# One core, one launch: a linear-attention scan and a gated feed-forward under a new order of work, with the flag of the general path tested early

## The chip, the cores and the metric

The kernel runs on one core of one Trainium2 chip. The core has a matrix engine (TensorE, "PE" in the profile, its weight loads "PEld"), a vector engine (VectorE, "DVE"), an activation engine (ScalarE, "ACT"), a general engine (GpSimd, "POOL") and a sync engine (SyncE, "SP"), which here issues all DMAs. Each engine runs its own list of instructions in order; they meet by semaphores. The metric is the device time of one execution in microseconds, and lower is better.

## The reference, cut to what matters

Eight heads of a gated linear attention with a complex decay, then a feed-forward block with a token shift and a sigmoid gate:

```python
mag = np.sqrt(a_re * a_re + a_im * a_im)
scale = np.minimum(mag, 0.999) / (mag + 1e-06)
a_re_n, a_im_n = (a_re * scale, a_im * scale)
for t in range(S):                       # S = 768, B = 4, H = 8, D = 48
    new_re = ar * S_re - ai * S_im       # ar, ai: row t of a_re_n, a_im_n
    new_im = ar * S_im + ai * S_re
    S_re, S_im = (new_re + k_t (x) v_t, new_im)
    y[:, :, t] = q_t . S_re
x_prev = x shifted by one token          # x = y, heads side by side: 384 wide
xk = mu_k * x + (1 - mu_k) * x_prev
xr = mu_r * x + (1 - mu_r) * x_prev
k = np.maximum(xk @ w_k, 0.0)            # 384 -> 1024
v = k * k @ w_v                          # 1024 -> 384
r = 1.0 / (1.0 + np.exp(-(xr @ w_r)))
return r * v
```

## The kernel before, in words

The sequence of each of the 4 batches is cut into two units of 384 tokens, so there are 8 units, u = 0 to 7. A unit passes through three stages.

The gate stage (`gate`, phase "g") loads the decays, keys and queries (`g<-in_gat`) and values (`v<-in_vt`), and turns the decays into cumulative logarithms and phases on ACT and DVE: exponentials, logarithms, arctangent, sine, two scans. The results multiply keys and queries in place (`g<-g,sq`, L712, and `g<-g,r`, L757). On the way the last columns and sums go into a tile `stat` (copies L705 and L731, accumulations of ACT): they show whether the decays stay in the range in which this way of computing is exact.

The attention stage (`attend`, phase "a") transposes keys on PE (`tr`, L848; L912 in unit 0), copies them out on ACT (`kt`), forms the products of keys and values per 64 tokens (`up`, L881; L951 in unit 0), adds them up to states on DVE, forms scores within 64 tokens (`sc`, L998, L993), masks them on DVE (`pt`) and sums both parts into the output (`y`, L1039). ACT writes that to the unit's input of the feed-forward, `xt` (L1074), and small DMAs move the last heads' rows (`xt<-ys`).

The feed-forward stage (`mix`, phase "m") forms the two mixes of neighbouring tokens (`x`, L376 and L380 in unit 0), the gates (`z` with `zr` by ACT), the first projection (`z`, L421, L417 in unit 0), its squared ReLU (`r`, `h`, `hx`), the second projection (`o`, L506), and the product of gate and projection (`y<-o,zr`, L524), which SP stores (`out_t<-y`, L529). In all units but the first a float32 operand is split in two parts and each block takes three matmuls. In unit 0 the weights, which come packed (phases "f": fetch `raw`, "w": convert with `hx<-raw` L574 and `wx` L579, "s": split), are used whole.

Phase "x" holds 48 steps of two matmuls on a tile of zeros (`room<-idle`, L1128), whose result nobody reads. The first 25 steps have widths of 512 to 256 columns, the others 384.

No loop orders the work. Each step registers itself with what it reads and writes, and a table `ORDER` gives each step of each phase its place in one list of 1652 steps. `Plan.run` sorts by the places, checks that each step stands behind what it depends on, and emits them; so the table sets the order on each engine's list, on the DMA queue of SP, and in which buffer a tile lies (`HOMES`). Nothing is scheduled after that.

After the list the kernel compares `stat` with limits (`lim`, written by memsets of POOL at the end), sums the comparisons over partitions by a matmul (`n`, L1168), writes an integer flag `bad` (L1169), loads it into a register of each engine (`nc.values_load`, L1172) and branches on it (L1173). Where the flag is set, a slow general path computes everything again, token by token; with these inputs it isn't set, and the branch jumps over that code.

Of the kernel before, what the change touches and what calls it, by code (L numbers as in the profile page):

```python
# [13 lines left out]
I32 = mybir.dt.int32  # L14
# [155 lines left out]
}  # L170
PIECE = 2
HB = 2
XB = 3
GB = 2
VB = 4
# [1098 lines left out]
```

## Time and profile before

| what | us |
|---|---|
| median of 3 runs (lowest to highest) | 408.85 (408.64 to 409.87) |
| the profiled execution: its time | 409.39 |
| its span, first to last instruction | 407.6 |
| time around the span | 1.79 |
| PE busy | 385.6 (95% of the span), 5801 matmuls |
| DVE busy, ACT busy | 319.2 (78%), 312.9 (77%) |
| mean granted clock of PE | 0.971 of 2.4 GHz |

The busy time of PE is counted from modelled ends of matmuls that overlap, so a busy PE isn't a PE at its peak. Times in the rows are microseconds from the span's start. In a row of busy shares each digit stands for a fortieth of the span, about 10.2 us. "Idle before" names what ended an engine's wait; "issue" means that nothing in the profile ended it.

### The profile page before, as it was taken

Reading aid. Unit: us, or ns where it says so; the run is one execution under the profiler, and the core shown is the slowest. Engines: PE = TensorE matmul, PEld = TensorE weight load, DVE = VectorE, ACT = ScalarE, POOL = GpSimd, SP = SyncE. Lnnn points to the kernel's source line nnn. Section 1 sums busy time; section 2 is a strip of 40 time slices with the busy share of each in tenths; the row PEclk is TensorE's granted clock in tenths of the full one; section 3 lists DMA queues with packets and bytes.
Section 4 is the critical chain, followed back from the end, with each engine's and each line's share of the span. In section 5 each row is a group of like instructions: output and inputs, shape, how many; then the busy total and the mean of one; then the engine's idle time right before and its main releaser. Section 6 shows DMA issues by size and latency. Waiting matters only on the chain.

```text
span 407.6 us, 13560 instructions
## 1 busy us (share of the span) xinstructions
PE 385.6 (95%) x5801; PEld 352.1 (86%) x5801; DVE 319.2 (78%) x516; ACT 312.9 (77%) x617; POOL 8.8 (2%) x32
## 2 busy tenths in 40 slices
PE   7769999999999999999999999999999999999993
PEld 6658865686798989999999989999999998999992
DVE  2996889899998799988997889969886955444352
ACT  6998999999999789899996988699767634152430
POOL 6000000000000000000000000000000000000000
PEclk9955999999999999999999999999999999999998
DMA  7987491514553515454144643344311332100101
GB/s 269 414 285 185 150 357 59 125 42 143 179 146 97 219 45 127 159 181 92 34 126 132 191 110 112 84 160 121 65 62 46 67 82 50 37 0 2 58 1 65
DMA packets 22994, 49.70 MB, mean 122 GB/s; under 512 B 4848, under 2 KB 16368, under 8 KB 22928
## 3 DMA queue, kind: packets, MB, share of 16 engines
q1 hardware_dynamic: 22928, 48.78, 39.2%
q8 instruction: 47, 0.77, 0.8%
q14 instruction: 19, 0.16, 0.1%
HBM read 31.06 MB, written 4.72 MB: 88 GB/s over the span
## 4 chain that ended last, share of the span: by engine, by line
PE 85%; DVE 6%; ACT 3%; issue 2%; DMA 2%; SPq 0%; DVEq 0%; ACTq 0%
PE z L421 28%; PE o L506 24%; PE y L1039 9%; PE sc L998 6%; PE up L881 5%; PE z L417 5%; PE tr L848 3%; DVE g L757 2%; PE sc L993 2%; PE up L951 1%; PE tr L912 1%; PE room L1128 1%; DMA g<-in_gat 1%; DMA xt<-ys 1%; DVE ph L722 1%
## 5 line engine op out<-in xcount | busy, mean ns | idle before, releaser
L421 PE MATMUL z<-x,w 128*128 128x384 f32 x693 | 127.3, 338 | 0.0
L421 PEld LDWEIGHTS z<-x,w 128*128 128x128 f32 x693 | 120.0, 188 | 1.2 <-ACT zr L285 0.2
L506 PE MATMUL o<-hx,w 128*128 128x384 f32 x504 | 96.0, 340 | 0.8 <-issue 0.7
L506 PEld LDWEIGHTS o<-hx,w 128*128 128x128 f32 x504 | 86.8, 188 | 2.1 <-issue 1.0
L278 ACT ACT_TABLE_LOAD x37 | 47.5, 1283 | 1.5 <-PEq L1263 0.8
L757 DVE TENSOR_TENSOR g<-g,r 128x768 f32<-128x768 f32 (+1 forms) x24 | 41.8, 1755 | 8.5 <-ACT r L285 7.9
L463 ACT ACTIVATE r<-z 128x384 f32<-128x384 f32 x64 | 31.0, 492 | 14.7 <-PE z L421 11.4
L467 ACT ACTIVATE h<-r 128x384 f32<-128x384 f32 x64 | 33.5, 528 | 9.4 <-DMA out_t<-y 4.7
L479 DVE TENSOR_TENSOR hx<-h,hx 128x384 fp32r<-128x384 f32 x56 | 30.5, 554 | 2.0 <-ACT hx L473 1.0
L394 ACT CAST x<-xm 128x384 fp32r<-128x384 f32 x42 | 21.3, 518 | 11.8 <-DVE xm L386 9.1
L397 DVE TENSOR_TENSOR x<-xm,x 128x384 fp32r<-128x384 f32 x42 | 22.9, 552 | 8.3 <-ACT x L394 8.0
L475 DVE CAST hx<-h 128x384 fp32r<-128x384 f32 x44 | 15.5, 355 | 17.5 <-PE o L506 9.8
L285 ACT ACTIVATE sq<-m 128x1152 f32<-128x1152 f32 (+1 forms) x30 | 28.1, 968 | 1.3 <-DVE m L681 1.2
L998 PE MATMUL sc<-g 48*64 48x64 f32 x1200 | 26.9, 234 | 0.8 <-issue 0.7
L998 PEld LDWEIGHTS sc<-g 48*64 48x64 f32 x1200 | 24.4, 143 | 3.4 <-issue 2.2
L891 DVE TENSOR_TENSOR state<-up,state 112x384 f32<-112x384 f32 x35 | 19.4, 553 | 9.4 <-PE up L881 8.2
L1074 ACT ACTIVATE xt<-y 112x192 f32<-112x192 f32 (+2 forms) x36 | 14.3, 396 | 15.4 <-PE y L1039 13.9
L1039 PE MATMUL y<-q,state 112*64 112x64 f32 (+1 forms) x704 | 25.3, 227 | 0.7 <-issue 0.7
L1039 PEld LDWEIGHTS y<-q,state 112*64 112x64 f32 (+1 forms) x704 | 23.0, 134 | 3.3 <-issue 2.3
L386 DVE SCALAR_TENSOR_TENSOR xm<-dx,mu_sb,xt 128x384 f32<-128x384 f32 x42 | 25.5, 614 | 0.4
L285 ACT ACTIVATE zr<-z 128x384 f32<-128x384 f32 x24 | 11.3, 490 | 17.2 <-PE z L421 17.2
L881 PEld LDWEIGHTS up<-v,kt 64*48 64x48 f32 (+1 forms) x1216 | 20.9, 127 | 3.7 <-issue 1.5
(87 smaller groups left out, 582.9 us busy)
## 6 DMA issues: line engine op xcount, KB each, us to landing
g<-in_gat SPq DMA_DIRECT2D x18, 768.0 KB, 6.5
raw<-in_w_all SPq DMA_DIRECT2D x9, 767.8 KB, 8.2
g<-in_gat SPq DMA_DIRECT2D x12, 384.0 KB, 4.4
v<-in_vt SPq DMA_DIRECT2D x24, 192.0 KB, 3.1
out_t<-y SPq DMA_DIRECT2D x24, 192.0 KB, 2.0
q<-g SPq DMA_DIRECT2D x84, 48.0 KB, 2.3
q<-g SPq DMA_DIRECT2D x28, 144.0 KB, 2.9
q<-g SPq DMA_DIRECT2D x40, 72.0 KB, 2.8
```

The lines of the kernel that those rows point to most:

```text
L278: nc.scalar.add_instruction(mybir.InstLoadActFuncSet(name=nc.get_next_instruction_name(), act_func_set_id=n, engine=mybir.EngineType.Activ ...
L285: nc.scalar.activation(out=out, in_=in_, func=func, **kw)
L386: nc.vector.scalar_tensor_tensor(out=xm[which, ct], in0=d[ct], scalar=mu_sb[:, which, ct:ct + 1], in1=X[u][:, ct, 0:U], op0=ALU.mult, op1= ...
L421: nc.tensor.matmul(z, lhsT=wt[s[0]][:, part, s[1]], rhs=r[which][:, ct], start=n == 0, stop=n == 3 * NT - 1)
L463: nc.scalar.activation(out=t["r", j], in_=t["f", j], func=AF.Relu, scale=1.0 / W_SCALE)
L467: nc.scalar.activation(out=t["h", j], in_=t["r", j], func=AF.Square)
L479: nc.vector.tensor_tensor(out=t["lo", j], in0=t["h", j], in1=t["hi", j].bitcast(F32), op=ALU.subtract)
L506: nc.tensor.matmul(tiles["o", mt], lhsT=w, rhs=r, start=j == 0 and n == 0, stop=j == NJ - 1 and n == len(parts) - 1)
L757: nc.vector.tensor_tensor(out=g[:, d, 2 * i:2 * i + 2], in0=g[:, d, 2:4], in1=t["r"][:, 1 - i, d].unsqueeze(2).to_broadcast([P, k, 2, U]), ...
L881: nc.tensor.matmul(t["up", c, s][i * HR:(KR if i else HR), h * D:(h + 1) * D], lhsT=keys, rhs=V[u][c][r, h * D:(h + 1) * D], start=True, s ...
L998: nc.tensor.matmul(y, lhsT=g[:, 2 * i, q], rhs=g[:, 2 * i + 1, q], start=i == 0, stop=i == 1)
L1039: nc.tensor.matmul(t["y", team][s][rows, h // 2 - team[0], c], lhsT=lhsT[:, cols], rhs=rhs, start=(s, h % 2) not in begun, stop=stop)
```

## The change

It does three things.

First, `ORDER` and `HOMES` are other numbers throughout: the list has three steps more, and nearly every step has another place in it. One line of the table before and after:

```diff
-    ("x", 0): (21, 26, 29, 32, 36, 40, 43, 46, 48, 51, 53, 55, 56, 58, 62, 64, 67, 69, 70, 72, 74, 76, 78, 82, 84, 87,
+    ("x", 0): (66, 77, 69, 25, 182, 84, 92, 102, 56, 269, 75, 41, 74, 110, 32, 46, 272, 37, 136, 82, 145, 98, 175, 63,
```

The fill steps are no longer in the order of their widths. On PE, at the start (`tr`, `sc`, `up`: the attention of unit 0), the list was:

```order
L912 MATMUL tr<-ident,g 128x128 x6
L998 MATMUL sc<-g 64x64 x24
L951 MATMUL up<-v,kt 64x48 x2
...
L951 MATMUL up<-v,kt 48x48 x2
L912 MATMUL tr<-ident,g 128x128 x3
L998 MATMUL sc<-g 64x64 x24
L912 MATMUL tr<-ident,g 128x128 x9
L951 MATMUL up<-v,kt_316 64x48 x2
```

and is now:

```order
L924 MATMUL tr<-ident,g 128x128 x6
L1010 MATMUL sc<-g 64x64 x24
L924 MATMUL tr<-ident,g 128x128 x3
L1140 MATMUL room<-idle 128x320 x2
L1140 MATMUL room<-idle 128x384 x2
L1140 MATMUL room<-idle 128x512 x2
...
L963 MATMUL up<-v,kt 64x48 x2
...
L963 MATMUL up<-v,kt 48x48 x2
L1140 MATMUL room<-idle 128x384 x4
L924 MATMUL tr<-ident,g 128x128 x9
```

Ahead of these rows stand 70 fill matmuls in both lists. Of the other 26, two, 14 and 10 stood in three groups, two behind the first `y` product, 14 ahead of the last one and 10 behind it; now there are groups of eight, four, two and two in this stretch, none until the last `y` of unit 0, and 10 behind it, ahead of the first feed-forward.

On ACT, where the sines of unit 0 end and the first keys are copied out (`r` are phases, `kt` transposed keys, `hx<-raw` a weight conversion), the list was:

```order
L745 ACTIVATE r<-r 128x384
L285 ACTIVATE r<-r,half_pi 128x384
L919 COPY kt<-tr 128x384
L926 COPY kt_316<-tr 128x3x2x16
L574 CAST hx<-raw 128x768
```

and is now:

```order
L757 ACTIVATE r<-r 128x384
L586 CAST hx<-raw 128x768
L290 ACTIVATE r<-r,half_pi 128x384
L290 ACTIVATE r<-r 128x384
L757 ACTIVATE r<-r 128x384
L931 COPY kt<-tr 128x384
```

One conversion has moved from behind the first copy of keys to a place ahead of it.

Second, the test of `stat` becomes steps of the list (phase "z": `look`), and the copies into `stat` are free to stand anywhere ahead of it. When 40 steps of the list are left, all of the last feed-forward, the flag is loaded on every engine and a branch hint is placed with it. On PE, near the end of the last unit, the list was:

```order
L421 MATMUL z<-x,w 128x384 x9
L506 MATMUL o<-hx,w 128x384 x3
L1168 MATMUL n<-ones_79,good 1x1
L1172 TENSOR_LOAD bad
L1173 COMPARE_AND_BRANCH
```

and is now:

```order
L1174 MATMUL n<-ones_79,good 1x1
L518 MATMUL o<-hx,w 128x384 x9
L433 MATMUL z<-x,w 128x384 x18
L518 MATMUL o<-hx,w 128x384 x9
L1184 TENSOR_LOAD bad
L1291 BRANCH_PREFETCH_HINT
L518 MATMUL o<-hx,w 128x384 x27
L433 MATMUL z<-x,w 128x384 x9
L518 MATMUL o<-hx,w 128x384 x24
L433 MATMUL z<-x,w 128x384 x18
L518 MATMUL o<-hx,w 128x384 x3
L1194 COMPARE_AND_BRANCH
```

The load and the hint now stand 81 matmuls ahead of the branch.

Third, the limits are written at the program's start, by ten memsets of POOL that stand ahead of the memset of `idle`, and a scratch size for DMA descriptors is set smaller.

```diff
 PIECE = 2
+LOAD = 40
+HINTED = (mybir.EngineType.PE, mybir.EngineType.DVE, mybir.EngineType.Activation, mybir.EngineType.SP, mybir.EngineType.Pool)
...
             emit()
             done.add(i)
+            if self.late and len(order) - len(done) == self.late[0]:
+                assert all(self.ops[j][2][0] == "m" for j in range(len(order)) if j not in done)
+                self.late[1]()
...
     nc.gpsimd.memset(ones1, 1.0)
+    lim = keep.tile([P, 2, ST_ALL], F32, name="lim")
+    for lo, hi, a, e in ((-2.0 ** 100, 2.0 ** 100, ST_X, ST_SQ), (0.0, 2.0 ** 20, ST_SQ, ST_L),
+                         (L_MIN, L0, ST_L, ST_PHI), (0.0, 1.0 / RE_MIN, ST_RE, ST_ALL),
+                         (-64.0, 64.0, ST_PHI, ST_RE)):
+        nc.gpsimd.memset(lim[:, 0, a:e], lo)
+        nc.gpsimd.memset(lim[:, 1, a:e], hi)
+    bad = keep.tile([1, 1], I32, name="bad")
     idle = keep.tile([P, 512], F32R, name="idle")
...
+        flag = []
+
+        def look():
+            good = keep.tile([P, 1], F32, name="good")
+            t, sn = {}, slot("ps")
+
+            def test():
+                ok = keep.tile([P, 2, ST_ALL], F32, name="ok")
+                nc.vector.tensor_tensor(out=ok[:, 0], in0=stat, in1=lim[:, 0], op=ALU.is_ge)
+                nc.vector.tensor_tensor(out=ok[:, 1], in0=stat, in1=lim[:, 1], op=ALU.is_le)
+                nc.vector.tensor_reduce(out=good, in_=ok, axis=mybir.AxisListType.XY, op=ALU.add)
+
+            def total():
+                t["n"] = bank(sn, "n")[:1, :1]
+                nc.tensor.matmul(t["n"], lhsT=good, rhs=ones1, start=True, stop=True)
+
+            def judge():
+                nc.vector.tensor_single_scalar(out=bad, in_=t["n"], scalar=2.0 * P * ST_ALL - 0.5, op=ALU.is_lt)
...
+        def load():
+            flag.append(nc.values_load(bad, min_val=0, max_val=1))
+            tc.mark_branch_hint_location("general", flag[0], engines=HINTED)
+
+        run([look], ("z", 0))
         with tc.manual_schedule():
             load_table(6)
+            plan[0].late = LOAD, load
             plan[0].homes = HOMES
             plan[0].run(ORDER)
...
-    flag = nc.values_load(bad, min_val=0, max_val=1)
-    with tc.If(flag > 0):
+    with tc.If(flag[0] > 0, label="general"):
...
-    nc = bacc.Bacc("TRN2", target_bir_lowering=False, num_devices=1)
+    nc = bacc.Bacc("TRN2", target_bir_lowering=False, num_devices=1, dynamic_dma_scratch_size=8192)
```

## Rows read from the trace of the kernel before

**Rows 1.** The page: busy tenths of PE and DVE in 40 slices.

```profile
PE   7769999999999999999999999999999999999993
DVE  2996889899998799988997889969886955444352
```

**Rows 2.** Stretches: length, busy of PE, PEld, DVE, ACT, POOL, clock, DMA share, GB/s.

```profile
24.31:51.57 27.26, 25.16 (x592) 21.95 (x593) 21.97 (x48) 24.41 (x53) 0.00 (x0) 0.67 0.62 176
...
53.28:400.72 347.44, 342.51 (x5126) 314.01 (x5125) 279.22 (x436) 266.21 (x516) 1.97 (x14) 1.00 0.35 102
```

**Rows 3.** Waits of PE, 53.28 to 400.72: total us, times, longest.

```profile
PE y L1039 <- issue: 1.6, 3, 0.7
PE z L417 <- DVE x L380: 0.9, 1, 0.9
PE sc L998 <- issue: 0.7, 1, 0.7
PE o L506 <- issue: 0.7, 1, 0.7
PE tr L848 <- DVE g L757: 0.6, 1, 0.6
PE z L417 <- DVE state L891: 0.2, 1, 0.2
```

**Rows 4.** Stretches of one microsecond, columns as in Rows 2.

```profile
22.00:23.00 1.00, 0.00 (x0) 0.00 (x0) 1.00 (x2) 1.00 (x4) 0.00 (x0) 0.52 1.05 424
42.00:43.00 1.00, 1.00 (x32) 0.93 (x33) 0.90 (x5) 1.00 (x4) 0.00 (x0) 0.74 0.17 68
```

**Rows 5.** Timeline of PE at the start: start, length, instructions, idle before.

```profile
2.65 15.09 PE L1128 MATMUL room<-idle 128*128 128x512 f32 x70 [2.65 <-POOL idle L328]
23.37 0.90 PE L912 MATMUL tr<-ident,g 128*128 128x128 f32 x3 [5.63 <-DVE g L757]
```

**Rows 6.** The chain that ended last: start, length, what, instructions.

```profile
31.55 2.12 PE tr L912 x9
...
35.98 2.09 PE y L1039 x41
38.07 0.94 PE room L1128 x2
...
44.64 1.22 PE y L1039 x38
...
47.64 2.64 PE room L1128 x14
...
189.15 1.31 PE tr L848 x12
```

**Rows 7.** The branch at line 1173: ns shortest/median/longest, start.

```profile
L1173 ACTq COMPARE_BRANCH  x1: 50/50/50, 401.9 to 401.9; - x1
...
L1173 PEldq COMPARE_BRANCH  x1: 3802/3802/3802, 402.0 to 402.0; - x1
```

**Rows 8.** The flag's load at line 1172, columns as in Rows 7.

```profile
L1172 DVEq TENSOR_LOAD <-bad x1: 545/545/545, 401.4 to 401.4; - x1
L1172 PEldq TENSOR_LOAD <-bad x1: 487/487/487, 401.4 to 401.4; - x1
```

**Rows 9.** Timeline of DVE at the end: the last product.

```profile
400.76 0.56 DVE L524 SCALAR_TENSOR_TENSOR y<-o,zr 128x384 f32<-128x384 f32 x1
```

**Rows 10.** DMA issues from 395 us on: KB each, median us to landing.

```profile
out_t<-y SPq DMA_DIRECT2D x3, 192.0 KB, 1.9
```

**Rows 11.** Groups by line: the weight conversion, busy us, mean ns.

```profile
L574 ACT CAST hx<-raw 128x768 f16<-128x768 bf16 (+1 forms) x10 | 10.1, 1023 | 0.0
```

**Rows 12.** Groups by line: one of the two lines of limits.

```profile
L1160 POOL MEMSET lim<- 128x24 f32 (+2 forms) x5 | 0.6, 133 | 16.7 <-PE sc L998 16.7
```

**Rows 13.** Timeline of POOL at the start: the statistics' zeroing.

```profile
2.54 0.27 POOL L331 MEMSET stat<- 128x208 f32 x1
```

**Rows 14.** Timeline of ACT at the start: the first accumulation.

```profile
5.38 0.52 ACT L285 ACTIVATE ph<-m 128x384 f32<-128x384 f32 x1
```

More of the change, by code (lines that the diff above doesn't have):

```diff
@@ L194 @@
     "g": "01010101",
-    "hx": "0100101010101010010010101010101010101010100110101010110101",
-    "kt": "001010010110110101101101",
+    "hx": "0110101010101010100101010111010101101011010010010100101101",
+    "kt": "010101010101110010110101",
     "ps": (
-        "400123230221232413134014143002041302310304102042111343104224341042421031010420124323313402434013"
-        "014302023040411232421032111301314213012410403232424032402434314013101232042120342034233010201342"
-        "32430042302411334102410101240432032124310344014304113044130324"
+        "320123321041320241400442323024023024211431223030440131423030134324243420241342031340303120123402"
+        "321301213113030044204230400340213400230442340112301204130134314022023142410313030341411321421040"
+        "010243121324043143243120132211331013342402340243104042324020314"
     ),
-    "pt": "01000110100101100101100110011010",
+    "pt": "01001001100110100110100101010110",
     "r": (
-        "021301201230131210102123032103210310203021131320211320312230302031231023123223010112130310211220"
-        "21031032030132100203313112310123200230321130203103203102"
-    ),
-    "v": "120310023102103021301210",
-    "x": "021011122021200011201012022102102022120102022102120011021021102",
+        "023110210231022303112102021102102102010212031312120301202101030210230012303031101212203210132001"
+        "30231031212130112030212303021013021221331033213021321203"
+    ),
+    "v": "130201312102130021301021",
+    "x": "021011201210211201211021022102200120022100210210210200210201200",
 }
@@ L219, in __init__ @@
     def __init__(self):
-        self.ops, self.data, self.slots, self.phase, self.homes = [], {}, {}, None, {}
+        self.ops, self.data, self.slots, self.phase, self.homes, self.late = [], {}, {}, None, {}, {}
     def slot(self, tag):
@@ L1147, in tile_kernel @@
                 run(gate(u + 2), ("g", u + 2))
+        flag = []
[12 more added lines that the diff above has]
+                nc.vector.tensor_single_scalar(out=bad, in_=t["n"], scalar=2.0 * P * ST_ALL - 0.5, op=ALU.is_lt)
+            op_dve(1260, test, reads=[(k, u, i) for k in ("L", "phi", "X") for u in range(NU) for i in range(NT)],
+                   writes=[("good",)])
+            op_pe(0.1, total, reads=[("good",)], writes=[("n",)], uses=[sn])
+            op_dve(4, judge, reads=[("n",)], writes=[("bad",)], uses=[sn])
@@ L1148, in tile_kernel @@
+        def load():
+            flag.append(nc.values_load(bad, min_val=0, max_val=1))
+            tc.mark_branch_hint_location("general", flag[0], engines=HINTED)
+        run([look], ("z", 0))
         with tc.manual_schedule():
             load_table(6)
+            plan[0].late = LOAD, load
             plan[0].homes = HOMES
             plan[0].run(ORDER)
-    bad = keep.tile([1, 1], I32, name="bad")
-    with pool("fin") as fin:
-        lim = fin.tile([P, 2, ST_ALL], F32, name="lim")
-        for lo, hi, a, e in ((-2.0 ** 100, 2.0 ** 100, ST_X, ST_SQ), (0.0, 2.0 ** 20, ST_SQ, ST_L),
-                             (L_MIN, L0, ST_L, ST_PHI), (0.0, 1.0 / RE_MIN, ST_RE, ST_ALL),
-                             (-64.0, 64.0, ST_PHI, ST_RE)):
-            nc.gpsimd.memset(lim[:, 0, a:e], lo)
-            nc.gpsimd.memset(lim[:, 1, a:e], hi)
-        ok = fin.tile([P, 2, ST_ALL], F32, name="ok")
-        nc.vector.tensor_tensor(out=ok[:, 0], in0=stat, in1=lim[:, 0], op=ALU.is_ge)
-        nc.vector.tensor_tensor(out=ok[:, 1], in0=stat, in1=lim[:, 1], op=ALU.is_le)
-        good = fin.tile([P, 1], F32, name="good")
-        nc.vector.tensor_reduce(out=good, in_=ok, axis=mybir.AxisListType.XY, op=ALU.add)
-        n = ps.tile([P, 512], F32, tag="ps0", name="n")[:1, :1]
-        nc.tensor.matmul(n, lhsT=good, rhs=ones1, start=True, stop=True)
-        nc.vector.tensor_single_scalar(out=bad, in_=n, scalar=2.0 * P * ST_ALL - 0.5, op=ALU.is_lt)
```

240 rows, old and new, of the table ORDER are left out of this document.

## The prediction

> **What bounds the kernel now.** I read the strips of the page first: TensorE (PE) is busy nine tenths or more in nearly all slices after the sixth, and VectorE (DVE) thins out to three to five tenths in the last eight [rows 1]. Then the table by stretches: between the first matmul of the first feed-forward (53.28 us) and the last one (400.72 us) PE is busy 342.51 of 347.44 us, so this stretch is PE work and only 4.93 us of it are gaps [rows 2]. The waits of PE in that stretch say whose the gaps are: 0.9 + 0.6 + 0.2 = 1.7 us are waits for DVE, and 1.6 + 0.7 + 0.7 = 3.0 us are "issue", which no other engine ends [rows 3]. An order of work can win at most the 1.7. That leaves two places outside: the start, 53.28 us in which PE also waits and runs slow, and the end, 407.6 - 400.72 = 6.9 us after the last matmul.
>
> In the start the granted clock leaves 2.4 GHz in the 23rd microsecond and comes back in the 43rd (means 0.52 and 0.74 of these two slices) [rows 4]; ahead of the fall PE had run 70 fill matmuls up to 17.74 us (2.65 + 15.09) and then stood 5.63 us until the first transpose's operand came from DVE [rows 5]. From there the chain of waits runs through PE almost without a break [rows 6]. ScalarE (ACT) is close behind: between its first copy of transposed keys and its last copies of the unit's output (24.31 to 51.57 us) it is busy 24.41 of 27.26 us [rows 2].
>
> **The end.** PE's branch over the general path takes 3802 ns, from 402.0 to 405.8 us, ACT's 50 ns [rows 7]; all that follows waits for PE. The flag is loaded only at 401.4 us [rows 8]. [...] What is late next is the last store: DVE's last product ends at 400.76 + 0.56 = 401.32 us [rows 9], and a store lands 1.9 us after its issue [rows 10], so 403.2 us. The end of PE's branch, 405.8, is thus replaced by 403.2 as the latest event, 2.6 us sooner; I take 2.5, since the stores are issued one after another. Against it: the load of 487 ns [rows 8] now stands among PE's matmuls. It costs nothing if queued matmuls cover it and 0.55 us if PE drains and restarts; I take 0.3. Behind it on PE stand 54 matmuls of the second projection and 27 of the gates. It waits for the flag, but DVE writes the flag ahead of the hidden tile that the nine matmuls before the load need, so no new wait. The sum matmul adds 0.1 to PE. On ACT and DVE the load (up to 545 ns [rows 8]) stands ahead of the next hidden tile, which PE needs only 9 matmuls later. On SP it stands ahead of the last three stores and is done long before them. The test itself (three DVE operations) was covered before by the wait for the last gate and is now in the thin stretch of DVE [rows 1]: nothing. Sum of the end: -2.5 + 0.3 + 0.1 = **-2.1 us**, from -2.6 (with a free load) to, if the hint gives nothing, +0.65.
>
> **The start.** The number of fill matmuls stays 96, and 70 still stand ahead. The other 26 move: before 2, 14 and 10; now 8, 4, 2 and 2 between transposes, scores and state products, and 10 ahead of the first feed-forward. If the clock stays high, PE saves on the small work: nine transposes take 2.12 us at the low clock and twelve 1.31 us at the high one, which is 0.236 against 0.109 each, so 18 x 0.127 = 2.3 us; the first product with the state takes 2.09 us low and 1.22 us high, 0.9 us [rows 6]. The 16 moved fills cost 16 x 2.64 / 14 = 3.0 us at the high clock, and the 2 and 14 that go took 0.94 + 2.64 = 3.6 [rows 6]. PE alone would be 2.3 + 0.9 + 3.6 - 3.0 = 3.8 us sooner at the first feed-forward. But ACT has only 27.26 - 24.41 = 2.85 us of idle time to give there [rows 2], and a weight conversion of 1.02 us [rows 11] now stands ahead of its first copy of keys, which leaves 1.8. DVE and ACT otherwise do the same work in the same phases. I take **-1.2 us**, two thirds of 1.8, with -2.85 as the other end; the bad end is the second rival. The limits' memsets, ten of about 133 ns [rows 12], now stand on POOL ahead of the idle tile that the fills read, so the fills begin and end 0.5 to 1.3 us later. That by itself costs nothing: nobody waits for them, and it shortens the 5.63 us pause in front of the first transpose [rows 5]. The zeroing of the statistics behind them ended at 2.81 us [rows 13], now at about 4.1 at the latest, and ACT's first accumulation begins at 5.38 us [rows 14]. On SP's queue two of three early weight loads move behind the inputs of the first unit; no DVE or PE wait in the start is for those inputs, so I count nothing.
>
> **The middle.** Every row of the table moves, but the matmuls are the same 5126 [rows 2]. What can change is the 1.7 us of waits [rows 3] and new ones. I count **0**, from -1.7 (all gone) to +4.2: each of the seven later units meeting one wait like the 0.6 us of the transposes on DVE. The copies into the statistics, which nobody reads before the test, are short and DVE is not full there: nothing.
>
> The sum is made against the profiled execution, 409.39 us (span 407.6 and 1.8 around it), which lies 0.54 above the median of the runs shown, 408.85. 409.39 - 2.1 - 1.2 + 0 = 406.1; on the runs' scale **405.6 us**, 0.8% less.
>
> **Rivals.**
> [...]
>
> The clock falls all the same, and the fills stand on PE's path at the low rate. This is the case on the other side. [...] Price: 16 x 0.47 (0.94 us for two [rows 6]) = 7.5, less the 3.6 that go, less the 27.26 - 25.16 = 2.1 us that PE stood idle [rows 2], is 1.8; and if the clock is still low behind 42 us, three products with the state at 0.87 more and ten fills at 0.28 more add 5.4, so 7.2. With 4.5, the middle: 409.39 - 2.1 + 4.5 = 411.8, on the runs' scale 411.2. It decides if the clock is at 1.2 GHz when the group of eight runs. Against it: the pause ahead of the first transpose is shorter now and the eight come within a few microseconds of it. [...]
>
> The new order brings waits of its own in the middle: at +4.2, 409.39 - 3.3 + 4.2 = 410.3, on the runs' scale 409.8. For it: the order before leaves only 1.7 us of such waits, which most other orders would not. Against it: ACT and DVE are idle a fifth of that stretch (266.21 and 279.22 of 347.44 us busy [rows 2]).
>
> **Chances.** A change of less than 0.3% (1.2 us) can't be told from none, so same is 407.6 to 410.1. Forecast 0.62 (faster 0.58, same 0.04), its own range 403.6 to 407.4 by the ends of the start and a microsecond or so of the middle; no hint 0.10 (faster 0.03, same 0.07); low clock 0.14 (same 0.03, slower 0.11); waits 0.14 (faster 0.03, same 0.08, slower 0.03). Faster 0.64, same 0.22, slower 0.14. The range for 8 in 10 leaves out most of the low clock and the best ends of all three terms together: 402.8 to 409.8.
>
> **What would show it.** The end: PE's branch of some 50 ns instead of 3802, a span that ends some 2 us after the last store has landed, and a gap of under 0.6 us on PE at the load. The start: a granted clock of 1.00, or a low stretch much shorter than 20 us, and the first feed-forward matmul near 52 us. The middle: PE's waits for other engines of about 1.7 us. The forecast is wrong if PE's branch still takes microseconds, if the clock is low for 20 us or more, or if waits of PE for DVE or ACT in the middle exceed some 4 us.

## The result, and the profile after

The changed kernel is slower: 414.89 us, median of 6 runs (411.09 to 416.52), against 409.93 for the kernel before on the same chip (6 runs, 408.64 to 413.28). The ratio is 1.0103, 95% interval 1.0065 to 1.0142; 405.6 was predicted. The profiled execution took 411.09 us, the fastest of the six, so its trace shows less of the loss than a usual run has. Against the profiled execution before, its span is 1.8 us longer (409.4 against 407.6): the first feed-forward matmul comes 0.93 us sooner (52.35), the middle is 3.9 us longer (351.3 against 347.4), and what follows the last matmul, the tail, is 1.2 us shorter (5.7 against 6.9 us to the end of the span).

The strips answer to [rows 1], the stretch to [rows 2] (columns as there):

```profile
PE   6777889999998999999999999999999999999994
DVE  2998799899997899969995888879899853358241
...
52.35:403.64 351.29, 343.39 (x5127) 315.85 (x5127) 279.94 (x437) 263.89 (x514) 2.16 (x4) 1.00 0.34 99
```

The strips hardly differ; the sum does. The middle has 7.9 us of gaps now, 4.9 before. The waits of TensorE in it, the answer to [rows 3] (total us, times, longest; the seven rows left out are 0.5 us or less each):

```profile
PE y L1051 <- issue: 2.3, 4, 0.9
PE sc L1010 <- issue: 1.9, 2, 1.0
PE z L429 <- DVE x L392: 1.6, 2, 0.8
PE tr L860 <- issue: 1.0, 1, 1.0
```

With a fifth of 0.5, the "issue" rows are 5.7 us, 3.0 before. That is most of the growth, and it is the kind of wait that the prediction had set aside as fixed.

The start on TensorE (start, length, instructions, idle before), to be laid beside [rows 5]:

```profile
3.29 14.61 PE L1140 MATMUL room<-idle 128*128 128x384 f32 x70 [3.29 <-POOL idle L340]
23.26 0.90 PE L924 MATMUL tr<-ident,g 128*128 128x128 f32 x3 [5.36 <-DVE g L769]
...
37.84 1.07 PE L1051 MATMUL y<-q,state 112*64 112x64 f32 x20 [1.43 <-DMA q<-g]
43.16 0.77 PE L1051 MATMUL y<-q,state 112*64 112x64 f32 x20 [0.96 <-ACT q L819]
52.35 0.88 PE L429 MATMUL z<-x,wx 128*128 128x384 f32 x2 [0.79 <-DVE x L392]
```

and its clock, the seventh value after the stretch, to be laid beside [rows 4]:

```profile
21.30:28.10 6.80, 4.68 (x60) 3.84 (x61) 6.59 (x11) 6.72 (x14) 0.00 (x0) 0.50 0.96 354
28.10:38.30 10.20, 7.61 (x181) 6.20 (x181) 8.97 (x20) 10.07 (x21) 0.00 (x0) 1.00 0.93 242
38.30:41.70 3.40, 3.40 (x118) 3.25 (x116) 2.32 (x3) 1.78 (x7) 0.00 (x0) 0.50 0.92 273
```

The clock was at 0.50 for 10.2 us instead of 20.5 (22.0 to 42.5 us in the trace before). That looks like the forecast, but it is no mark of the new start: in a trace of the old start (the old order with the flag, below) it was low for 10.2 us as well, in two stretches:

```profile
22.20:28.90 6.70, 5.34 (x105) 4.19 (x105) 6.46 (x12) 6.67 (x14) 0.00 (x0) 0.50 0.97 303
...
42.60:46.00 3.40, 3.40 (x88) 3.17 (x91) 1.78 (x4) 1.77 (x2) 0.00 (x0) 0.50 0.52 135
```

The new start also has waits that the old one did not have: the first `y` products wait 1.43 us for a copy of queries (`q<-g`, a DMA) and 0.96 us for ScalarE.

The end, the branch at line 1194 and what follows it, to be laid beside [rows 7] (ns shortest/median/longest, start):

```profile
L1194 SPq EVENT_SEMAPHORE  x8: 17/17/17, 407.4 to 408.0; - x8
L1194 PEldq COMPARE_BRANCH  x1: 3900/3900/3900, 400.4 to 400.4; - x1
...
L1194 DVEq COMPARE_BRANCH  x1: 84/84/84, 403.8 to 403.8; - x1
...
L1194 SPq COMPARE_BRANCH  x1: 70/70/70, 404.7 to 404.7; - x1
L1194 DVEq EVENT_SEMAPHORE  x1: 21/21/21, 406.9 to 406.9; - x1
```

TensorE's branch takes 3900 ns with the hint, 3802 before. Its sequencer reaches the branch at 400.4 us, while matmuls are queued until 403.6, so that stall is mostly covered now. The rows to see are others. VectorE's branch ends at 403.9, and its next instruction comes at 406.9. SP's branch ends at 404.8, and its next instruction, the first of the eight semaphores, comes at 407.4. Both rows of the branch show under 0.1 us, and yet each engine stands some three microseconds behind it. SP is the last: the span ends 1.9 us behind its first semaphore here, and 1.9 us behind it in the trace before.

### The profile page after: what moved, and what is told of

The parts are those of the page before. It is cut to its first block, busy times and chain, and to the rows that moved or that the text cites. A ratio compares the mean times of both kernels' runs of the same rounds, so it can differ in the third digit from the quotient of the medians.

```text
span 409.4 us, 13559 instructions
## 1 busy us (share of the span) xinstructions
PE 382.2 (93%) x5801; PEld 350.3 (86%) x5801; DVE 320.6 (78%) x516; ACT 310.8 (76%) x616; POOL 9.6 (2%) x32
## 4 chain that ended last, share of the span: by engine, by line
PE 76%; ACT 9%; DMA 6%; DVE 4%; issue 2%; SPq 2%; DVEq 0%
PE z L433 28%; PE o L518 21%; PE y L1051 9%; PE up L893 5%; PE sc L1010 4%; PE tr L860 3%; PE z L429 3%; DMA raw<-in_w_all 2%; DMA g<-in_gat 2%; ACT sq L290 2%; PE sc L1005 2%; DVE g L769 2%; DMA q<-g 1%; ACT L283 1%; ACT r L290 1%
## 5 line engine op out<-in xcount | busy, mean ns | idle before, releaser
L518 PE MATMUL o<-hx,w 128*128 128x384 f32 x504 | 94.4, 339 | 0.0
L290 ACT ACTIVATE sq<-m 128x1152 f32<-128x1152 f32 (+1 forms) x30 | 27.8, 966 | 1.1 <-DVE m L693 1.0
L1051 PEld LDWEIGHTS y<-q,state 112*48 112x48 f32 (+1 forms) x704 | 22.4, 131 | 4.9 <-issue 4.1
L1026 DVE TENSOR_TENSOR pt<-sc,mask 128x384 f32<-128x384 f32 (+1 forms) x36 | 17.5, 505 | 9.9 <-PE sc L1005 5.4
L429 PE MATMUL z<-x,wx 128*128 128x384 f32 x66 | 22.8, 494 | 1.8 <-DVE x L392 1.6
L1140 PE MATMUL room<-idle 128*128 128x384 f32 (+4 forms) x96 | 20.7, 374 | 3.3 <-POOL idle L340 3.3
```

The lines of the kernel that those rows point to most:

```text
L290: nc.scalar.activation(out=out, in_=in_, func=func, **kw)
L429: nc.tensor.matmul(z, lhsT=wx[s[0]][:, s[1]], rhs=hi[which][:, ct], start=ct == 0, stop=ct == NT - 1)
L518: nc.tensor.matmul(tiles["o", mt], lhsT=w, rhs=r, start=j == 0 and n == 0, stop=j == NJ - 1 and n == len(parts) - 1)
L1051: nc.tensor.matmul(t["y", team][s][rows, h // 2 - team[0], c], lhsT=lhsT[:, cols], rhs=rhs, start=(s, h % 2) not in begun, stop=stop)
```

## The experiments

Theory 1 was that the new order makes TensorE wait longer at the ends of its instruction blocks. The rivals were that the flag's part costs the time, that the new start makes runs uneven, and that chance or the clock did it.

How the block ends are found: the page of the changed kernel has a queue of instructions with 47 packets and 0.77 MB, so 16.4 KB each (`q8 instruction: 47, 0.77`). Its first packet moves between 26.5 and 27 us, when 122 to 125 matmuls of TensorE have started, the 46th between 401 and 401.5 us, at 5787 to 5790: 45 steps of 126 matmuls on the mean. If the matmuls of a trace are numbered from its start, the waits of the changed kernel's middle that are of this kind stand at 1737, 1863, 2625, 3641, 4021, 5165, 5292, 5418: steps that are multiples of 127 within a few (one wait of 0.5 us put down to "issue", at 1064, stands off this grid). 127 matmuls with their weight loads are 254 instructions. That they fill one packet (a block), and that the waits stand where one block ends and the next begins, is the author's estimate from these two counts. In the trace of the changed kernel, a packet of this queue moves between 126.0 and 127.5 us (packets, MB, share of 16 engines):

```profile
q8 instruction: 1, 0.02, 3.9%
```

and right behind it TensorE stands for 0.90 us in the middle of 48 scores:

```profile
127.03 0.69 PE L1010 MATMUL sc<-g 48*64 48x64 f32 x24
128.62 0.73 PE L1010 MATMUL sc<-g 48*64 48x64 f32 x24 [0.90 <-issue]
```

The table below therefore sums, for the trace of each kernel, TensorE's gaps of over 0.2 us between the first feed-forward matmul and the last one, apart for those at numbers within six below and nine above the grid 1737 + 126.93 k (16 of 127 numbers, so chance would give an eighth) and all others.

Not every block end costs time. Counted over the twenty traces of the table, behind the first feed-forward matmul: of 179 block ends with twelve matmuls of 384 columns ahead of them, none has a gap of over 0.2 us; of 533 with twelve short ones (128 columns or fewer), 105 have one. What decides between the short ones, no run shows.

| kernel | first `z`, us | gaps at block ends | other gaps | middle, us | after last matmul | ratio to before (95%) |
|---|---|---|---|---|---|---|
| before | 53.3 | 3.0 | 1.5 | 347.4 | 6.9 | 1 |
| changed | 52.3 | 5.5 | 2.0 | 351.3 | 5.7 | 1.0103 (1.0065 to 1.0142) |
| new order alone | 54.2 | 6.8 | 1.8 | 353.6 | 6.6 | 1.0147 (1.0107 to 1.0187) |
| changed, no hints | 57.3 | 6.2 | 3.2 | 354.5 | 5.6 | 1.0104 (1.0068 to 1.0140) |
| old order with flag | 52.6 | 3.6 | 0.9 | 348.0 | 5.8 | 0.9980 (0.9951 to 1.0009) |
| new start, old rest | 56.6 | 3.5 | 1.8 | 347.3 | 7.1 | 1.0016 (0.9986 to 1.0047) |
| the same, loads moved, flag | 53.9 | 3.7 | 1.6 | 348.7 | 5.8 | 1.0034 (0.9996 to 1.0072) |
| old order, flag, 16 more | 52.1 | 3.7 | 1.6 | 348.8 | 5.8 | 1.0004 (0.9971 to 1.0037) |
| old order, flag, 24 more | 52.4 | 4.2 | 1.4 | 348.8 | 5.7 | 1.0033 (1.0003 to 1.0064) |
| old order, flag, 32 more | 52.0 | 2.4 | 1.6 | 347.7 | 5.8 | 0.9974 (0.9943 to 1.0005) |
| old order, flag, 40 more | 54.4 | 3.9 | 0.4 | 347.7 | 5.7 | 0.9960 (0.9928 to 0.9993) |
| before, 40 more | 52.7 | 4.1 | 0.6 | 347.2 | 7.2 | 0.9994 (0.9962 to 1.0026) |
| old order, flag, 64 more | 56.1 | 5.2 | 1.8 | 353.0 | 5.7 | 1.0104 (1.0057 to 1.0150) |
| old order, flag, 96 more | 66.9 | 5.5 | 0.9 | 350.1 | 5.7 | 1.0313 (1.0272 to 1.0355) |
| changed, 32 more | 57.0 | 3.2 | 2.2 | 348.0 | 5.7 | 1.0066 (1.0032 to 1.0100) |
| changed, 40 more | 56.4 | 5.7 | 0.9 | 350.8 | 5.7 | 1.0182 (1.0138 to 1.0226) |
| changed, 64 more | 57.6 | 5.5 | 2.9 | 353.2 | 5.7 | 1.0194 (1.0145 to 1.0242) |
| changed, 96 more | 62.1 | 5.5 | 3.4 | 354.0 | 5.7 | 1.0335 (1.0298 to 1.0371) |
| old start, new rest, flag | 52.9 | 6.3 | 5.4 | 359.8 | 5.7 | 1.0204 (1.0154 to 1.0253) |
| the same, 32 more | 53.0 | 4.6 | 3.5 | 353.1 | 5.7 | 1.0069 (1.0030 to 1.0108) |

"More" are extra matmuls that nothing uses (below). Each row's trace is one execution; the ratio is over six to twelve.

### The parts of the change, apart

The code of the kernel before with the new table alone:

```diff
-ORDER, HOMES of the kernel before
+ORDER, HOMES of the changed kernel, without the phase "z"
```

> The code of the kernel before with the new order and its buffers alone: no early flag, no hints, the test of the statistics at the end as before. Theory 1 (the loss lies in the new order's middle: longer waits at the ends of instruction blocks and more waits of TensorE for the other engines; in the two profiled executions the start won 0.93 us, the middle lost 3.85, the end won 1.1): without the end's gain this is the slowest kernel of all, the changed kernel plus about 1.1, 4 to 7 us over the kernel before (1.010 to 1.017). Rival 2 (the flag's part costs: its load, its hints, the earlier instruction stream): the order alone wins the start's 0.9 us and is 0.5 to 1.5 us under the kernel before (0.996 to 0.999). Rival 3 (chance of the run, the clock): no difference, 0.998 to 1.002.

Measured 417.1 us, 1.0147. That the order (with its buffers) costs the time holds, and the rivals don't; that it does so at block ends is what its trace says, with 6.8 us there against 3.0. By the ratios the flag's part takes 1.8 us off (1.0103 against 1.0147), but the two intervals overlap. The waits of TensorE in its trace, 54.24 to 407.92 us:

```profile
PE sc L1126 <- issue: 2.4, 4, 1.0
PE y L1167 <- issue: 2.4, 4, 0.8
PE tr L976 <- issue: 1.7, 1, 1.7
...
PE sc L1121 <- issue: 0.8, 1, 0.8
```

That is 7.3 us of issue waits. Behind one of them the clock fell. Four stretches around the wait of 1.7 us, columns as in [rows 2]:

```profile
240.00:243.50 3.50, 3.50 (x166) 3.03 (x165) 3.50 (x7) 2.88 (x6) 0.00 (x0) 1.00 0.53 120
243.50:245.10 1.60, 0.01 (x1) 0.00 (x0) 1.50 (x4) 0.51 (x1) 0.00 (x0) 1.00 0.44 92
245.10:248.50 3.40, 3.32 (x11) 3.32 (x11) 1.70 (x3) 1.30 (x2) 0.00 (x0) 0.50 0.47 113
248.50:252.00 3.50, 3.50 (x21) 3.50 (x21) 1.87 (x4) 0.31 (x1) 0.00 (x0) 1.00 0.13 47
```

TensorE stands for 1.6 us, and then the clock is at 0.50 for 3.4 us: 1.7 us more lost, an estimate from that share. The old order with the flag's part:

```diff
-    ("g", 7): (..., 1646, ...),
+    ("g", 7): (..., 1354, ...),
+    ("z", 0): (1575, 1607, 1609,),
```

> The old order with the flag's part alone: the copy of the last decay statistic moved forward, the test, its sum and the judgement at the places of the new kernel near the end, the load when 40 steps are left, with the hints. Theory 1: the end wins about 1.1 us as in the profiled executions, 0.996 to 0.998 of the kernel before, and TensorE's branch still takes about 3.9 us, beside matmuls that are queued. Rival 2 (the flag's part costs): 2 to 5 us slower, 1.005 to 1.012, and the loss shows as waits of engines near the load. As predicted before the result (the hint spares TensorE its 3.8 us): 0.994 to 0.996, and TensorE's branch is short.

Measured 409.91 us, 0.998. The interval holds 1, so 0.8 us is what the ratio says and not more; the tail of the trace is 1.1 us shorter, and it is short in every trace with the flag (5.6 to 5.8 us against 6.6 to 7.2). TensorE's branch took 3430 ns. And without the hints:

```diff
-            tc.mark_branch_hint_location("general", flag[0], engines=HINTED)
```

> The changed kernel without the five hints; the early load stays. Theory 1 (the hint changes nothing; TensorE's branch is as long with it as without): the same time as the changed kernel within 0.3%, 1.007 to 1.014 of the kernel before, TensorE's branch 3.8 to 3.9 us, the end 5.8 us behind the last matmul. If the hints cost time (rival 2: blocks fetched for them at a bad moment): 1 to 4 us faster than the changed kernel, 0.999 to 1.007. If the hints work on part of the engines: the end 1 to 3 us longer.

Measured 415.18 us, 1.0104: the hints change nothing that these runs can tell. The trace also tells the two engines at the end apart:

```profile
L1193 SPq EVENT_SEMAPHORE  x8: 17/17/17, 413.4 to 416.0; - x8
...
L1193 DVEq EVENT_SEMAPHORE  x1: 21/21/21, 412.5 to 412.5; - x1
L1193 SPq COMPARE_BRANCH  x1: 50/50/50, 412.9 to 412.9; - x1
```

VectorE went on 0.5 us behind its branch, but SP stood all the same: its eight semaphores are spread over 413.4 to 416.0 us, with 2.1 us between the third and the fourth, and the tail is 5.6 us. So SP's pause is its own and not a wait for VectorE. The last part, the new order for the first 320 steps:

```diff
-ORDER of the kernel before, all steps
+ORDER of the changed kernel for its first 320 steps, the rest in the order before
```

> The code of the kernel before; the first 320 steps in the new order (all before the first matmuls of the feed-forward, the fill matmuls too), the rest in the old order. Theory 1: the start wins 0.9 us and the rest is as before, 0.997 to 0.999 of the kernel before. Rival (the new start is what makes executions uneven, by transfers of the first gates that land late): 1.002 to 1.012, with waits of TensorE for DMAs before the first feed-forward matmul and a spread of some us between executions.

Measured 411.45 us, 1.0016: no gain. The middle is the old one (347.3 us), but the first `z` came at 56.6 us, behind a wait of 3.64 us for the copy `q<-g`. The waits for that copy were 1.4, 2.6, 3.4 and 3.6 us in the four traces of the new start so far, and nil in the two of the old.

### The end of a block moved against the work

64 (32, 96, 16, 24, 40) matmuls of 128x16 on the zero tile, behind the last fill ahead of the first transpose, where TensorE waits for VectorE anyway. Up to 40 of them end ahead of that transpose, so they take no time from later work, but by the grid they shift where each later block ends:

```diff
+                for _ in range(SHIFT if i == LAST_FILL else 0):
+                    nc.tensor.matmul(room[0][:, :16], lhsT=idle[:, :P], rhs=idle[:, :16], start=True, stop=True)
```

> The changed kernel with 64 more matmuls of 128x16 in TensorE's idle time before its first transpose (they read the zero tile; nothing uses them). They add nothing to the work that follows, but move the ends of TensorE's 16 KB instruction blocks by half a block against the work. Theory A (TensorE runs dry at the block ends, where its next block is fetched while only short matmuls are queued): the waits that the view of waits calls issue stay on the same grid of matmul numbers (1737 plus or minus multiples of 127, the 64 counted), so they fall on other work; their sum changes by over 1 us from the 5.7 and 7.3 us of the two traces in the new order, up or down, and the middle with it. Theory B (the waits belong to the work, whatever the blocks): the same matmuls of the work wait as before (their numbers are 64 higher), the sum stays 5 to 8 us, and the time stays at 1.007 to 1.014 of the kernel before.

> The old order with the flag's part (the kernel of the experiment with the flag alone) and the same 64 matmuls of 128x16 before the first transpose. Theory A: the issue waits in the middle (3.7 us with the flag alone, 3.0 us in the kernel before) change by over 1 us and fall on other work; if the old order's middle owed its small sum to where its block ends fell, the middle grows by 2 to 4 us (1.003 to 1.009 of the kernel before). Theory A2 (the new order has more places at which short matmuls stand alone, wherever the blocks end): the sum stays 2 to 4 us, time 0.996 to 1.001. Theory B: the same work waits as before.

> As the run before, with 32 of the matmuls: a quarter of a block. Theory A: another set of places, and a sum of its own between 1 and 7 us; the time follows the sum, 0.993 to 1.007 of the kernel before. Theory A2: 2 to 4 us, 0.996 to 1.001. Theory B: the same work waits.

Measured 1.0194, 1.0104 and 0.9974. Theory A holds in its numbers and B falls: the waits stand on the same numbers and on other work. What makes TensorE stand there, a fetch or something else, no run shows. The old order, good until then, loses 5 us of its middle with 64 extra matmuls (353.0 us). The same place of the work in two traces of the old order, first with 40 extra matmuls, then with 64:

```profile
134.62 1.38 PE L1183 MATMUL y<-q,state 112*64 112x64 f32 x40
135.93 0.68 PE L1183 MATMUL y<-pt,v 64*64 64x64 f32 x28
137.40 0.54 PE L1183 MATMUL y<-pt,v 64*48 64x64 f32 x20 [0.79 <-issue]
137.87 1.85 PE L650 MATMUL o<-hx,w 128*128 128x384 f32 x9
```

```profile
136.66 1.38 PE L1183 MATMUL y<-q,state 112*64 112x64 f32 x40
137.96 0.33 PE L1183 MATMUL y<-pt,v 64*64 64x64 f32 x4
140.19 1.43 PE L1183 MATMUL y<-pt,v 64*48 64x64 f32 x44 [1.89 <-DVE ph L866]
```

The 48 products are cut behind the 28th in one and behind the 4th in the other: 24 matmuls earlier for 24 extra ones. The second cut is put down to VectorE, but the matmul has the number 1990 in both traces, which is on the grid, and that number has a gap in all seven traces of the old order with extra matmuls; the label names an event that only happened to come last. With 64 and 96 the extra matmuls also outlast the idle time and delay the start (in the old order the 64 ran until 27.8 us, the 96 until 34.7), so of those two only the middle is to be compared.

> The changed kernel with 32 of the extra matmuls of 128x16 before its first transpose: a quarter of an instruction block. So far the new order at shift 0 took 1.010 and at shift 64 1.019 of the kernel before, the old order with the flag 0.998, 0.997 (shift 32) and 1.010 (shift 64). Theory C (the two orders differ by nothing but the phase of their block ends against the work): over the four quarters the new order takes on the mean what the old one does, so here or at shift 96 it must come to 0.993 to 1.000, with a middle of 347 to 349 us. Theory D (the new order also has more places at which a block end finds nothing but short matmuls queued, and waits of its own): every phase of it stays over 1.004, the middle over 350 us.

> As the run before, three quarters of a block. Theory C: here or at shift 32 0.993 to 1.000 of the kernel before. Theory D: over 1.004, the middle over 350 us. By either theory the long issue waits stand at matmul numbers 1737 plus or minus multiples of 127, whatever work that is.

> The old order with the flag's part and 96 of the extra matmuls. Theory C: the old order too is bad at half of its phases, 1.004 to 1.012 of the kernel before, the middle over 350 us. Theory D: as at shifts 0 and 32, 0.995 to 1.001, the middle 347 to 349 us. The long issue waits at the same matmul numbers by either.

> The old order with the flag's part and 16 of the extra matmuls: between two phases that were good (0.998 and 0.997). If the sum of the waits changes slowly with the phase: 0.994 to 1.000, the middle 347 to 348.5 us. If single block ends decide (an end that falls some ten matmuls earlier meets other work): anything from 0.993 to 1.008. The best of these phases is the version to keep.

Measured 1.0066, 1.0335, 1.0313, 1.0004. With 32 extra matmuls the new order's middle is 348.0 us, as good as the old one's: a middle of that length was not out of its reach, against theory D. But at 0, 40, 64 and 96 it is 351 to 354 us, and the old order's is under 349 at 0, 16, 24, 32 and 40; so C, that only the phase (where the block ends fall in the work) differs, holds in part. What the new order with 32 still lacks lies, in its trace, in the start (57.0 us).

> The flag's part; the first 320 steps in the old order, the rest in the new order, no extra matmuls. The blocks then end at the same work of the middle as in the changed kernel. Theory C (phase): a middle of 351 to 354 us, with issue waits near the matmuls 1737, 1863, 3641, 4021, 5165 and 5292 as in the changed kernel, 1.006 to 1.012 of the kernel before. If the new middle is late only behind the new start: a middle of 348 us, 0.996 to 1.000.

> The same with 32 extra matmuls of 128x16 in the idle time before the first transpose (3.4 us of it, at 0.105 us each in the trace of the old order with 32). Theory C (phase alone): the middle falls to 347.5 to 349 us, and the whole is 2.5 to 5 us faster than its pair without them, 0.994 to 1.001 of the kernel before: useless work makes the kernel faster. Theory D (the new middle has losses of its own): within 1 us of its pair.

Measured 419.1 us (1.0204) and 413.23 us (1.0069). Adding 32 useless matmuls made the kernel 5.9 us faster. Neither reached the time that theory C gave, though: behind the old start the new rest has waits of its own in both, 1.9 us of transposes for ScalarE (`tr <- ACT r`, at the same work and so 32 numbers apart; in the second it happens to fall near a block end and is counted there) and 1.6 and 1.1 us for copies `q<-g`.

> The old order with the flag's part and 24 extra matmuls, between two phases that measured 1.000 (16) and 0.997 (32). Single block ends decide: 0.993 to 1.004; a slow change with the phase: 0.996 to 1.000.

> As the run before, 40 extra matmuls, between 0.997 (32) and a middle that was 5 us longer (64; its start was late too). Single block ends decide: 0.993 to 1.010; a slow change: 0.998 to 1.003.

> The kernel before with 40 extra matmuls of 128x16 in the idle time before the first transpose and nothing else: old order, late test of the statistics. If the phase alone made the 0.996: 0.995 to 0.998 of the kernel before. If the flag's part is worth the 0.9 us by which the tail is shorter in every trace with it (5.6 to 5.8 us against 6.5 to 6.8): 0.997 to 1.001, about 1 us over the kernel with both.

> The changed kernel with 40 extra matmuls. The new order measured 1.010, 1.007, 1.019 and 1.033 at shifts 0, 32, 64 and 96 (the last two with a late start). If a phase serves every order alike: 0.996 to 1.001. If each order has its own good phases, and the new one waits of its own besides (for the copies of the queries, 1.4 to 3.6 us in the start and 0.5 to 1.5 us near matmul 1064): 1.004 to 1.016, with issue waits within ten matmuls of the grid 1737 plus or minus multiples of 127.

Measured 1.0033, 0.9960, 0.9994, 1.0182. From 24 to 32 extra matmuls the ratio falls by 0.6%, and in the traces the gaps at block ends fall from 4.2 to 2.4 us: that speaks for single block ends as what decides, though the two ratios stand on different runs of the kernel before. The old order with the flag and 40 extra matmuls, 408.84 us, is the one version whose interval lies below both kernels, by 0.4% (0.1 to 0.7) and by 1.4%; as the best of eighteen versions tried, its 0.4% is in part chosen and may not come again. The phase alone gives 0.06%, not told from nothing. No phase serves every order: 40 is best for the old one and bad for the new.

The run with the kernel before and 40 extra matmuls also tells of the end. Its rows at the branch:

```profile
L1178 SPq EVENT_SEMAPHORE  x8: 17/17/17, 405.2 to 405.7; - x8
...
L1178 PEldq COMPARE_BRANCH  x1: 358/358/358, 401.2 to 401.2; - x1
...
L1178 SPq COMPARE_BRANCH  x1: 50/50/50, 401.9 to 401.9; - x1
```

TensorE's branch lost its 3.4 us by the shift alone, and the tail is 7.2 us, no shorter than before: SP stands behind its own branch from 401.9 to 405.2 us. So it is in all twelve traces with extra matmuls: TensorE's branch took 358 to 486 ns there, and with the flag's part the tail was 5.7 to 5.8 us, against 5.6 to 5.8 in the traces where the branch took microseconds.

### The weight loads in the new start

```diff
-    ("f", 4): (135,),  ("f", 6): (191,),  ("f", 7): (146,),  ("w", 7): (266, 291,),
+    ("f", 4): (62,),   ("f", 6): (216,),  ("f", 7): (214,),  ("w", 7): (289, 297,),
```

> The new order for the first 320 steps, the old order behind it, the flag's part; and of the new start three of the weight loads moved: the new order issues them between the copies that stack the first queries (rows 24, 27 and 36 of the SP queue), here one of them goes before those copies and two behind them, as in the old order, and one conversion of weights goes back behind its load. If the queries' copies land late because 1.5 MB loads are queued beside them (wait of 1.4 to 3.6 us of the first y matmuls for the DMA q<-g in all four traces of the new start, none in the two of the old): that wait is gone, the first feed-forward matmul comes 1.5 to 3.5 us earlier than in the traces of the new start (52.3 to 57.3 us), and the time is 0.990 to 0.997 of the kernel before. Rival (the new start is late for the order of VectorE's work, the copies are late whatever stands beside them): the wait stays over 1 us, 0.998 to 1.003.

Measured 411.18 us, 1.0034: a miss. The wait for the copies `q<-g` is gone, so the loads queued beside them made it; but 1.6 us of wait for ScalarE's copies of queries and 0.9 us for a load of values came in its place:

```profile
PE tr L1055 <- DVE g L900: 5.0, 2, 4.9
PE y L1182 <- ACT q L950: 1.6, 1, 1.6
PE up L1094 <- DMA v<-in_vt: 0.9, 1, 0.9
```

The first `z` came at 53.9 us, and the whole is not faster. What else the new start loses stays open.

## Why the prediction was wrong

**The middle, 0: the step that failed.** It took the 3.0 us of "issue" in [rows 3] as given ("an order of work can win at most the 1.7") and let only waits for engines grow. The issue waits were the part that moved. In the three traces with the new order throughout and no extra matmuls the middle is 3.9 to 7.1 us longer: 2.5 to 3.8 us at block ends, 0.3 to 1.7 in other gaps, and in the two longer ones 1.7 us of lowered clock behind a gap; the rest, up to 0.9, is longer busy time. (Behind the old start it was 12.4 us longer, of which 3.3 at block ends, 3.9 in other gaps and 3.4 by two stretches of lowered clock.) The bound of +4.2 us was near the smallest of these, for another reason than its own. Behind short matmuls 105 of the 533 block ends have gaps, of 0.2 to 1.9 us.

**The start, -1.2.** This trace gained 0.93 us, with the clock low for 10.2 us instead of 20.5, and both were luck. It was the best of six: with the new start and no or few extra matmuls the first `z` came at 52.3, 54.2, 57.3, 56.6, 57.0 and 56.4 us, with the old start at 52.0 to 54.4 in nine. The clock was low for 10.2 to 20.5 us in those six traces, and for 10.2 to 20.5 us in those nine: that the fills' new places shorten the low stretch is not shown. And "no DVE or PE wait in the start is for those inputs, so I count nothing" looked at the loads moved behind the inputs, and not at the three that now stand among the copies of queries. In whole times the new start is worth 1.0016, not told from nothing.

**The end, -2.1.** The 2.5 us in it stood for a branch of TensorE that the hint makes short. No run shows that a hint does so: the branch took 3900 ns with it, 3315 ns in the trace without hints and 3802 ns before, and in the changed kernel's trace no packet of the queue q8 moved between TensorE's hint at 386.9 us and its branch at 400.4. And the term was wrong at its root: "all that follows waits for PE" was read from PE's long row, but the end waited for SP. In the trace before, whose branch rows are [rows 7], SP's branch ends at 402.7 us, and its next instruction starts at 405.7:

```profile
L1173 SPq EVENT_SEMAPHORE  x8: 17/17/17, 405.7 to 406.2; - x8
...
L1173 SPq COMPARE_BRANCH  x1: 50/50/50, 402.7 to 402.7; - x1
```

The last store had landed at 403.2, as forecast, so SP did not wait for it. TensorE's branch ends at 405.8, so taking that away leaves SP's pause. Of the gain measured, 1.2 us of tail, 0.9 is that SP's branch ends 1.1 us behind the last matmul instead of 2.0, since the flag's load (540 ns on SP) and two short instructions no longer stand between the last store and the branch; the other 0.3 is a shorter pause of SP (2.7 against 3.0). What makes SP and VectorE pause behind a branch, no run took apart.

**The rivals.** Low clock in the start was not the cause: it was low for no longer than before, 10.2 to 20.5 us in six traces. (One run of the changed kernel, the slowest, had a mean granted clock of 0.921 against 0.974 to 0.985 in the other five; it has no trace.) New waits in the middle, put at 409.8 with a chance of 0.14, came nearest in kind; the low clock's 411.2 was nearer in time, by a cause that did not act.

## What to carry to other kernels

"Issue" in the waits of an engine is not a constant: number the instructions, see whether the gaps stand at equal steps (127 matmuls here), and expect any edit that adds, drops or reorders instructions to move them, by up to 5 us in 350 here. So compare two orders over several phases (a few useless instructions in an idle time shift them) before one is called better, and read several traces where runs spread by more than the difference. Before a long branch is removed, see whether another engine stands as long at the same jump: here TensorE's went from 3802 to 358 ns, and the tail from 6.9 to 7.2 us.

## What the runs showed that was not expected

- Useless matmuls made a kernel faster: 32 of 128x16, 413.2 against 419.1 us.
- A wait of 1.5 to 1.9 us, or two shorter ones close together, was in seven traces followed by 3.4 us at a clock of 0.50 (eight stretches); waits as long stood in other traces with no fall behind them.
- The branch of TensorE to the same place took 358 to 486 ns in thirteen of the twenty traces and 2270 to 4398 ns in the other seven, and the tail was no shorter for it.
- SP stood 2.1 to 3.3 us right behind its own branch, or up to three instructions further on, in all twenty traces.
- A load of one register took 463 to 722 ns, each hint 41 to 55 ns.
